# Filler matmuls placed by a shorter activity window, one K copy moved, and the closing flag put last, in a fused attention and gated-FFN kernel

## The chip, the cores and the metric

The kernel runs on one core of one Trainium2 chip. The metric is the device time of one execution in microseconds, as a median over several runs. A profiled execution gives a trace with the start and the length of every instruction of every engine; its span runs from the first to the last instruction. TensorE's clock is granted in steps, and the trace records the grant (1.0 is full speed, 0.5 half).

## What is computed

```python
xn = _layernorm(x)                       # x: 1 x 2048 x 512, bf16
q  = (xn @ wq) -> 32 heads of 16         # k, v: one head of 16 for all queries
scores = einsum("bhqd,bkd->bhqk", q, k) * 16 ** -0.5
p  = softmax(scores); o = p @ v
s  = o.reshape(...) @ wo
B  = (silu(x @ w_gate) * (x @ w_up)) @ w_down     # 1792 wide, here on xn
out = x + s * silu(B)
```

The scores are 32 heads x 2048 queries x 2048 keys, that is 134 million exponentials.

## The kernel before

**Tiles.** The score matrix is cut into 32 blocks (`NBLK`): 4 stretches of 512 queries, times 4 groups of 8 heads, times 2 halves of a group (4 heads). A block has 32 tiles of 128 keys by 2 heads by 512 queries, which is one PSUM pair of banks (128 x 1024 fp32). So there are 1024 tiles. Each tile is two score matmuls (line 877), which use 32 rows of the array each and run side by side, into one of three PSUM pairs `ring[0..2]`.

**Two engines share the exponentials.** `ring[0]` and `ring[1]` go to ScalarE, which takes 780 of the tiles with one ACTIVATE each (line 937) into one of eight buffers `Pb` (8 early tiles go into the still unused `g2_sb`, called `XB`). `ring[2]` goes to VectorE, which makes the exponential of the other 244 out of integer bit operations: a pass out of PSUM per tile (line 991), and three per two tiles (lines 1005, 1010, 1017). The products with V (line 747) are groups of four matmuls in four column strips, summed in the bank `o_ps`. The FFN, the Q projections and the output projection use the bank `m_ps`, also in groups of four (line 488).

**The order is planned in Python.** Class `_Sched` is a list scheduler that plays the engines forward with fixed costs (exponential on ScalarE 0.904 us, a group of four matmuls or one tile of scores `MMF` = 0.215, VectorE's pass out of PSUM 1.135). `pe_pick` chooses TensorE's next step: a score tile for ScalarE, a score tile for VectorE, a waiting group of another kind, or a filler. The planned order is then written out and pinned for each engine with order-only dependencies (`chain`); the semaphores come from the tile framework. Nothing is reordered at run time: each engine runs its own list and waits for data.

**Fillers.** There are three kinds. `junk` is one matmul of the identity into `ring[2]`'s second bank, used early only. `zero` is a group of four matmuls with a zero stationary operand (`zw`) that adds zero to the sums in `o_ps`. `mzero` adds zero to an open sum in `m_ps`. A filler is taken only when the plan has a gap of at least `MMF` on TensorE and `activity(F)`, the planned TensorE work in the last 3.4 us, is under `ACTMIN` = 1.7 (or, for one special case, `ACTLOW` = 1.5). A score tile counts 0.107 there, transposes (`tr`) and the narrow V projections (`vmm`, 16 columns) count nothing, everything else its length.

**Prologue.** Rows arrive in four chunks of 512. For each chunk VectorE takes statistics (lines 437, 438), GpSimd the power -1/2 (line 444), VectorE the normalised rows (447); TensorE transposes them (452); ScalarE and VectorE copy the transposes out (458); TensorE makes K (461, later 488) and V (469), and VectorE copies K out twice, masked for even and odd heads, into `KT[0]` and `KT[1]` (465). For chunk 0 these copies come in halves of 256 keys: `ke0` and `kf0` are the first half into `KT[0]` and `KT[1]`.

**Tail.** After the last exponential the sums of the last block are copied out (line 760), transposed on TensorE (1045), divided by the denominators (1053 to 1055), transposed back (1331), copied by ScalarE (1333) and multiplied by `wo` for the last four row tiles (488). VectorE multiplies by the gate (690); the residual is added by GpSimd for two row tiles and by VectorE for two (695); SyncE issues one store each (698). Beside that a flag is made: VectorE checks that the denominators lie in range (1335 to 1338), TensorE sums the result over the partitions (1343), VectorE compares (1356), and each engine loads the flag into a register (1363) and branches (1364). With the flag set, a slow exact path would redo the result; it is not taken for these inputs. All stores and the input loads go through SyncE's own queue, which issues in order.

Of the kernel before, what the change touches and what calls it, by code (L numbers as in the profile page):

```python
# [14 lines left out]
ALU = mybir.AluOpType  # L15
AX = mybir.AxisListType
# [5 lines left out]
GRP = 32  # L22
# [8 lines left out]
NWARM, NJUNK = 13, 200  # L31
D_START, D_LIM, D_LIM_END = 26, 12, 8
F_ON, F_OFF = 26, 60
PB_URG, AHEAD, LAZY, ACTMIN, ACTLOW = 6, 16, 8, 1.7, 1.5
DPRI, DTOL, DWIN = -1.0, 0.12, 0.15
TOL, MERGE, KE, KB, KR, PW = 0.17, 0.1, 1000, 3.0, 16, 2.0

# [246 lines left out]
def kernel(  # L284
# [13 lines left out]
    nc = tc.nc  # L298
    S, D, H, F = _dims(A_x, A_wq, B_w_gate)
# [38 lines left out]
    xnT = persist.tile([P, KC, S], BF16, name="xnT")  # L338
# [14 lines left out]
    ring = [psum.tile([P, 1024], FP32, name=f"ring{i}") for i in range(3)]  # L353
    o_ps = psum.tile([P, 512], FP32, name="o_ps")
    m_ps = psum.tile([P, 512], FP32, name="m_ps")
# [33 lines left out]
    zw = sb([P, GRP], BF16, "zw")  # L389
# [74 lines left out]
    def e_kev(t0, t1, src, half):  # L464
        return nc.vector.tensor_scalar(out=KT[half][:, t0:t1], in0=src, scalar1=hmask[:, half:half + 1],
                                       scalar2=None, op0=ALU.mult)
# [27 lines left out]
    def OP(eng, dur, deps, emit, prio, mode=None, name=""):  # L494
        return sd.new(_Op(eng, dur, deps, emit, prio, mode, name))
# [110 lines left out]
    ke1 = OP("DVE", 0.34, [ka1], lambda: e_kev(H2, 512, bank["o"][:, 0:H2], 0), (0.21, 0), name="kev")  # L606
    brel["2a"] = qe1
    pro_v(0, evs, "2a", 0.4)
    kf0 = OP("DVE", 0.34, [ka0, ke0], lambda: e_kev(0, H2, bank["m"][:, 0:H2], 1), (0.9, 0), name="kev")
    kf1 = OP("DVE", 0.34, [ka1, ke1], lambda: e_kev(H2, 512, bank["o"][:, 0:H2], 1), (0.25, 1), name="kev")  # L610
    brel["m"], brel["o"] = kf0, kf1
    q_ready[0] = [qe0, qe1]
# [76 lines left out]
    def e_out_mul(n, src, dst):  # L689
        return nc.vector.scalar_tensor_tensor(out=dst[:, :D], in0=src, scalar=0.25, in1=g2_sb[:, n, :],  # L690
                                              op0=ALU.mult, op1=ALU.mult)
# [5 lines left out]
    def e_out_st(n):  # L697
        return nc.sync.dma_start(out=out_v[:, n, :], in_=res[n % 4][:, :D])
# [121 lines left out]
    def act_block():  # L820
        b = cur["ba"]
        while b < NBLK and rem(b, 0) + rem(b, 1) == 0:
            b += 1
        return b if b < NBLK else None
# [309 lines left out]
    def activity(F):  # L1134
        a = 0.0
        for o in reversed(sd.pe_log):
            if o.start < F - 3.4:
                break
            a += 0.107 if o.name == "sc" else 0.0 if o.name in ("tr", "vmm") else o.dur
        return a  # L1140

    def pe_pick():
        F = sd.free["PE"]
        ready = sd.ready["PE"]
        ts = None
        b = now_block()
        rel = [i for i in (0, 1) if slot[i].start is not None]
        if b is not None and rel:
            i = min(rel, key=lambda i: sd.avail(slot[i], "PE"))
            x = act_x(b)  # L1150
            tr_ = tile_ready(b, x)
            if tr_ is not None:
                ts = max(F, sd.avail(slot[i], "PE"), tr_)
        td = None
        if d_ok() and slot[2].start is not None:
            rd = max(F, sd.avail(slot[2], "PE"))
            dt = dve_tile(1 - act_x(b) if b is not None else 0)
            if dt is not None:
                r_ = tile_ready(*dt)
                if r_ is not None:  # L1160
                    td = max(rd, r_)
        tm = None
        if ready:
            tm = max(F, min(o.ready for o in ready))
            now = [o for o in ready if o.ready <= tm + 1e-9]
            outst = cur["nA"] - sum(1 for o in pb_rel[-2 * NPB:] if o is not None and o.start is not None) \
                - max(0, len(pb_rel) - 2 * NPB)
            ba = act_block()

            def rank(o):  # L1170
                if o.name in ("pv", "dpv"):
                    fin = ba is None or o.prio[1] < ba
                    if fin or outst >= PB_URG:
                        return (0, o.prio)
                    return (1 if o.name == "dpv" else 3, o.prio)
                if o.mode == "f" or o.name == "pmm":
                    return (0.5, o.prio)
                if o.name == "part":
                    return (4, o.prio)
                return (0.8 if ahead() < LAZY else 3.5, (o.seq,))  # L1180
            co = min(now, key=lambda o: (rank(o), o.seq))
        cands = []
        if ts is not None:
            cands.append(ts)
        if tm is not None:
            if ts is None or tm + sd.switch(co.mode) + co.dur <= ts + TOL:
                cands.append(tm)
            else:
                tm = None
        if td is not None and (ts is None or td + sd.switch("r") + MMF <= ts + DTOL):  # L1190
            back = max(sd.free["DVE"] - F, 0.0) + sum(o.dur for o in sd.ready["DVE"])
            if back < DPRI and td <= F + DWIN:
                return td, ("dve", dt)
            td = None
        else:
            td = None
        junk = cur["np"] == 0 and cur["pair"] is None and cur["junk"] < NJUNK and all(
            w.start is None or v.start is not None and v.end + 0.13 <= F for w, v, bk in held if bk == "2b")
        if not cands:
            return (F, ("junk", None)) if junk else None  # L1200
        T = min(cands)
        zb = act_block()
        zb = NBLK - 1 if zb is None else zb
        act_ = activity(F)
        Tz = ts if act_ < ACTLOW and ts is not None and tm is not None and co.mode == "f" else T
        if Tz - F >= MMF + sd.switch("c") and (act_ < ACTMIN or cur["issued"] == NTILE):
            for bb in (zb - 1, zb):
                if bb >= 0 and oev[bb].start is None and oev[bb - 1].start is not None \
                        and sd.avail(oev[bb - 1], "PE") <= F and blk_pv[bb] and oev[bb].left > 0 and (bb not in fin_b or any(o.start is None for o in blk_pv[bb])):
                    return F, ("zero", bb)  # L1210
            if cur.get("mo"):
                return F, ("mzero", None)
        if junk and T - F > 0.3:
            return F, ("junk", None)
        if ts is not None and ts <= T + 1e-9:
            return ts, ("act", i)
        if tm is not None and tm <= T + 1e-9:
            return tm, ("op", co)
        return td, ("dve", dt)

    def d_ok():
        return cur["issued"] >= D_START and planned(d_gate)

    def pe_do(start, what):
# [4 lines left out]
                cur["mo"] = m_open[id(arg)]  # L1229
            return  # L1230
        if kind == "mzero":
            o = _Op("PE", MMF, [], lambda: [nc.tensor.matmul(
                out=m_ps[GRP * g:GRP * g + GRP, :], lhsT=zw[:], rhs=xnT[:, 0, 0:512], start=False, stop=False,
                tile_position=(0, GRP * g)) for g in range(4)], (0,), "c", "zero")
            o.seq = sd.seq
            sd.seq += 1
            sd.place(o, start)
            return
# [74 lines left out]
    def tadd(eng, ins):  # L1313
        chain(eng, ins)
# [1 line left out]
    la, lb = sorted((0, 1), key=lambda i: slot[i].seq)  # L1316
    assert job["part"] and job["partm"]
    st["obank"].append(f"{la}a")
    tq01, tq23 = ring[lb][:, 0:512], ring[lb][:, 512:1024]
    tp = [ring[la][:, 512:1024], o_ps[:]]  # L1320
    tadd("PE", e_out_mm(LN + 3, bank[st["obank"][3]][:, :D], range(NQ - 1)))
    tadd("PE", tq_emit(1, [0, 1], tq01))
    tadd("PE", tq_emit(1, [2, 3], tq23))
# [10 lines left out]
    dlf = dl[:].rearrange("p h q g o -> p (h q g o)")  # L1334
    tadd("DVE", nc.vector.tensor_scalar(out=dlc[:], in0=dlf, scalar1=DEN_LO, scalar2=DEN_HI, op0=ALU.max, op1=ALU.min))
    tadd("DVE", nc.vector.tensor_tensor(out=dlc[:], in0=dlc[:], in1=dlf, op=ALU.is_equal))
    tadd("DVE", nc.vector.tensor_reduce(out=fmin[:, 2:3], in_=dlc[:], axis=AX.X, op=ALU.min))
    tadd("DVE", nc.vector.tensor_reduce(out=fmin[:, 3:4], in_=fmin[:, 0:3], axis=AX.X, op=ALU.min))
    dsts = [ab[0], ab[1], oa[(LB + 1) % 4], oa[(LB + 2) % 4]]
    obk = [bank[k][:, :D] for k in st["obank"]]  # L1340
    for k in range(2):
        tadd("PE", e_out_mm(LN + k, obk[k], [NQ - 1]))
    tadd("PE", nc.tensor.matmul(out=tq01[0:1, 0:1], lhsT=fmin[:, 3:4], rhs=ones_f[:], start=True, stop=True))
    for k in range(2, 4):
        tadd("PE", e_out_mm(LN + k, obk[k], [NQ - 1]))

    def fin_add(k, eng, nm):
        tadd(nm, e_out_add(LN + k, dsts[k], eng))
        tadd("SP", e_out_st(LN + k))

    tadd("DVE", e_out_mul(LN, obk[0], dsts[0]))
    fin_add(0, nc.gpsimd, "POOL")
    tadd("DVE", e_out_mul(LN + 1, obk[1], dsts[1]))
    fin_add(1, nc.gpsimd, "POOL")
    tadd("DVE", e_out_mul(LN + 2, obk[2], dsts[2]))
    tadd("DVE", nc.vector.tensor_single_scalar(out=flag_i[:], in_=tq01[0:1, 0:1], scalar=P - 0.5, op=ALU.is_lt))
    tadd("DVE", e_out_mul(LN + 3, obk[3], dsts[3]))
    fin_add(2, nc.vector, "DVE")
    fin_add(3, nc.vector, "DVE")
    MAIN.close()  # L1360


# [34 lines left out]
```

## Time and profile before

| | |
|---|---|
| five runs, us | 784.9, 785.5, 786.14, 790.17, 792.85 (median 786.14) |
| the profiled execution's own time | 790.22 us |
| its span, first to last instruction | 788.4 us |
| mean granted TensorE clock | 0.981 |
| busy: ScalarE, VectorE, TensorE, GpSimd | 758.8, 732.3, 706.4, 50.4 us |
| ScalarE exponentials | 780 of about 1.14 us each; they overlap, and follow each other every 0.92 us |
| fillers on TensorE | 44 groups of four with zeros in `o_ps`, 7 `junk` |

The profile is a page of tables about one execution, and a trace that can be asked for more: groups of instructions by source line, waits, stretches of time, and instructions in order of time. TensorE is PE, its weight loads PEld, VectorE DVE, ScalarE ACT, GpSimd POOL, SyncE SP. A `q` behind an engine means its sequencer (waits, branches, DMA issue). "Busy" of a matmul includes its pipeline, so a busy PE is not PE at its peak.

### The profile page before, as it was taken

To read this page: it belongs to the slowest core of one execution; us is meant where nothing else is said; L and a number is where in the kernel's file an instruction comes from. 1 tells how busy PE (TensorE), PEld (TensorE's weight loads), DVE (VectorE), ACT (ScalarE), POOL (GpSimd) and SP (SyncE) were. 2 spreads that over 40 slices of the span, in tenths; PEclk is the share of its full clock that TensorE was granted. 3 is DMA by queue.
4 is the path that set the end of the run, shared out by engine and by line. 5 is a ranking of instruction groups with operands and counts; after the bars stand their busy time and mean duration, and the time that the engine had idled before them with its cause. 6 is when DMAs were issued, how large, how long until landed. Compare 5 with 4: busy or idle time off the path is not lost.

```text
span 788.4 us, 19587 instructions
## 1 busy us (share of the span) xinstructions
PE 706.4 (90%) x8170; PEld 210.4 (27%) x8172; DVE 732.3 (93%) x920; ACT 758.8 (96%) x866; POOL 50.4 (6%) x59
## 2 busy tenths in 40 slices
PE   8999888899989889899989898899988989899994
PEld 3322222222222222222222222222222222222221
DVE  7569999999989999999999999999999999999994
ACT  6889999999999999999999999999999999999993
POOL 2100000000011000000002000000000301000001
PEclk9689999999999999999999999999999999999998
DMA  9300000000011000000001000000000000000001
GB/s 328 122 22 1 23 2 15 10 2 23 3 30 42 16 15 2 22 3 10 16 18 33 29 22 2 12 13 9 17 1 23 29 23 2 1 23 2 22 2 32
DMA packets 21192, 20.09 MB, mean 25 GB/s; under 512 B 8744, under 2 KB 17192, under 8 KB 21096
## 3 DMA queue, kind: packets, MB, share of 16 engines
q1 hardware_dynamic: 19512, 18.20, 7.7%
q8 instruction: 66, 1.08, 0.6%
q10 hardware_dynamic: 1584, 0.56, 0.3%
q14 instruction: 30, 0.25, 0.1%
HBM read 14.19 MB, written 2.34 MB: 21 GB/s over the span
## 4 chain that ended last, share of the span: by engine, by line
ACT 53%; PE 28%; issue 12%; DVE 7%; DMA 0%; SPq 0%; ACTq 0%; POOL 0%; DVEq 0%; POOLq 0%
ACT Pb L937 46%; PE ring L877 10%; PE m_ps L488 10%; PE o_ps L747 5%; ACT th L657 4%; DVE Bf L991 2%; ACT th L674 1%; PE ring L433 1%; ACT g_sb L937 1%; DVE x_sb L1010 1%; DVE Bf L1010 1%; PE ring L452 0%; DVE Bf L1017 0%; DVE Bf L1005 0%; DVE x_sb L991 0%
## 5 line engine op out<-in xcount | busy, mean ns | idle before, releaser
L937 ACT ACTIVATE Pb<-ring 128x1024 bf16<-128x1024 f32 x772 | 727.0, 1136 | 8.7 <-PE ring L877 8.4
L877 PE MATMUL ring<-QB,KT 32*128 32x512 bf16 x2048 | 308.6, 387 | 60.0 <-ACT Pb L937 57.1
L991 DVE TENSOR_SCALAR Bf<-ring 128x1024 uint16<-128x1024 f32 x172 | 209.8, 1220 | 11.5 <-PE ring L877 9.7
L877 PEld LDWEIGHTS <-KT 32*128 32x128 bf16 x2048 | 92.9, 91 | 353.0 <-issue 348.9
L747 PE MATMUL o_ps<-Pb,VA 128*32 128x512 bf16 x1544 | 148.9, 388 | 0.0
L1010 DVE TENSOR_TENSOR Bf<-Bf,Bf 128x2048 f16<-128x2048 f16 x74 | 90.2, 1218 | 0.1
L991 DVE TENSOR_SCALAR x_sb<-ring 128x1024 uint16<-128x1024 f32 x72 | 87.9, 1220 | 2.4 <-PE ring L877 2.2
L488 PE MATMUL m_ps<-xnT,wu_sb 128*32 128x512 bf16 x896 | 72.8, 388 | 5.2 <-DVE ab L659 5.2
L488 PE MATMUL m_ps<-wd_sb,hT 128*32 128x512 bf16 x896 | 71.5, 383 | 1.2 <-DVE g_sb L676 1.2
L488 PE MATMUL m_ps<-xnT,wg_sb 128*32 128x512 bf16 x896 | 71.7, 385 | 0.0
L747 PE MATMUL o_ps<-Bf,VD 128*32 128x512 f16 x688 | 67.9, 387 | 0.9 <-DVE Bf L1017 0.6
L732 POOL TENSOR_TENSOR oT<-oa,rb 128x512 bf16<-128x512 f32 x15 | 20.5, 1364 | 616.3 <-DMA rb<-dscr 569.1
L1017 DVE TENSOR_SCALAR Bf<-Bf 128x2048 uint16<-128x2048 uint16 x86 | 59.2, 689 | 0.5
L747 PEld LDWEIGHTS <-VA 128*32 128x32 bf16 x1560 | 38.4, 94 | 51.5 <-issue 49.9
L1005 DVE TENSOR_SCALAR Bf<-Bf 128x2048 uint16<-128x2048 uint16 x74 | 50.6, 689 | 0.0
L659 DVE SCALAR_TENSOR_TENSOR ab<-th,m_ps 128x512 f32<-128x512 f32 x56 | 38.1, 681 | 3.4 <-ACT th L657 3.3
L663 DVE TENSOR_TENSOR hT<-ab,m_ps 128x512 bf16<-128x512 f32 x56 | 38.2, 682 | 2.5 <-PE m_ps L488 2.4
L657 ACT ACTIVATE th<-m_ps 128x512 f32<-128x512 f32 x56 | 39.8, 710 | 0.0
L747 PEld LDWEIGHTS <-VD 128*32 128x32 f16 x976 | 26.1, 94 | 41.2 <-issue 38.0
L1010 DVE TENSOR_TENSOR x_sb<-x_sb 128x2048 f16<-128x2048 f16 x24 | 30.3, 1264 | 0.0
L747 PE MATMUL o_ps<-x_sb,VD 128*32 128x512 f16 x288 | 28.0, 386 | 1.1 <-DVE x_sb L1010 0.9
L488 PEld LDWEIGHTS <-wu_sb 128*32 128x32 bf16 x896 | 19.1, 95 | 34.3 <-issue 30.5
(115 smaller groups left out, 387.9 us busy)
## 6 DMA issues: line engine op xcount, KB each, us to landing
rb<-dscr SPq DMA_DIRECT2D x15, 256.0 KB
out_dram<-xn SPq DMA_DIRECT2D x16, 128.0 KB, 1.7
dn<-oa SPq DMA_DIRECT2D x120, 2.0 KB, 1.7
oa<-oa SPq DMA_DIRECT2D x60, 32.0 KB, 2.0
wg_sb<-in_B_w_gate_dram SPq DMA_DIRECT2D x1, 1792.0 KB, 11.5
wu_sb<-in_B_w_up_dram SPq DMA_DIRECT2D x1, 1792.0 KB
wd_sb<-in_B_w_down_dram SPq DMA_DIRECT2D x1, 1792.0 KB, 20.4
x_sb<-in_A_x_dram SPq DMA_DIRECT2D x3, 512.0 KB
```

The costliest lines, as they stand in the source:

```text
L488: return [nc.tensor.matmul(out=dst[GRP * j:GRP * j + GRP, :], lhsT=w[:, GRP * j:GRP * j + GRP], rhs=rhs, start=start, stop=stop, tile_posi ...
L657: t_ = OP("ACT", 0.477, [a], lambda: nc.scalar.activation(out=th[i][:], in_=m_ps[:], func=ACT.Tanh, scale=0.5), (0,), name="tanh")
L659: s_ = OP("DVE", 0.6, [t_, ab_rel[i]], lambda: nc.vector.scalar_tensor_tensor(out=ab[i][:], in0=th[i][:], scalar=1.0, in1=m_ps[:], op0=ALU ...
L663: h = OP("DVE", 0.6, [b], lambda: nc.vector.tensor_tensor(out=hT[:, f, :], in0=ab[i][:], in1=m_ps[:], op=ALU.mult), (1,), name="hmul")
L732: return [pk, q], lambda eng: eng.tensor_tensor(out=oT[qs % 2][:, jj, :], in0=o0[:], in1=rbt[:], op=ALU.mult)
L747: r.append(nc.tensor.matmul(out=o_ps[GRP * g:GRP * g + GRP, :], lhsT=lhs, rhs=rhs, start=(n == 0), stop=(n == pv_total[(b, g)] - 1), tile_ ...
L877: return lambda: [nc.tensor.matmul(out=ring[sl][:, u * 512:(u + 1) * 512], lhsT=KT[half][GRP * g:GRP * g + GRP, t * P:(t + 1) * P], rhs=QB ...
L937: lambda: nc.scalar.activation(out=buf, in_=ring[i][:], func=ACT.Exp, scale=escale, bias=ebias),
L991: lambda: nc.vector.tensor_scalar(out=U[:, hs], in0=ring[si][:], scalar1=ubias, scalar2=UINF, op0=ALU.add, op1=ALU.min), (1.5, u), name="p ...
L1005: o1 = OP("DVE", 0.6, [pa, pa0] + wrel, lambda: nc.vector.tensor_scalar(out=Bf[wi], in0=U, scalar1=0x3FF, scalar2=0x3800, op0=ALU.bitwise_and,
L1010: return lambda: eng.tensor_tensor(out=Bf[wi][:, a:z].bitcast(FP16), in0=Bf[wi][:, a:z].bitcast(FP16), in1=U[:, a:z].bitcast(FP16), op=ALU ...
L1017: o2 = OP("DVE", 0.6, o3, lambda: nc.vector.tensor_scalar(out=U, in0=U, scalar1=0x7C00, scalar2=None, op0=ALU.bitwise_and), (2, u, 1), nam ...
```

## The change

It has five parts. (1) The planner looks back over 1.8 us in place of 3.4, and asks for 0.95 (or 0.8) of planned work in place of 1.7 (or 1.5). (2) When VectorE's score bank is free in the plan, and VectorE tiles have begun, a new filler writes zero groups into `ring[2]`'s second bank (a sum of its own, begun and closed by each group). (3) `kf0`, the copy of the first 256 keys into `KT[1]`, is planned after the last transposes of chunk 0 have been copied out. (4) In the tail the second pair of transposes goes to `o_ps` and the second transposes back go to `ring[lb]`'s second bank (the two have changed places). (5) In the tail GpSimd adds row tiles 0 and 2 and VectorE 1 and 3 (before: 0, 1 and 2, 3); the four stores stand together ahead of the flag; the flag's last two reductions, its matmul and its comparison come after the last addition.

```diff
-PB_URG, AHEAD, LAZY, ACTMIN, ACTLOW = 6, 16, 8, 1.7, 1.5
+PB_URG, AHEAD, LAZY, ACTMIN, ACTLOW = 6, 16, 8, 0.95, 0.8
...
-    kf0 = OP("DVE", 0.34, [ka0, ke0], lambda: e_kev(0, H2, bank["m"][:, 0:H2], 1), (0.9, 0), name="kev")
+    kf0 = OP("DVE", 0.34, [ka0, ke0, evs[3]], lambda: e_kev(0, H2, bank["m"][:, 0:H2], 1), (0.9, 0), name="kev")
...
-            if o.start < F - 3.4:
+            if o.start < F - 1.8:
                 break
...
             if cur.get("mo"):
+                return F, ("mzero", m_ps)
+            if d_ok() and slot[2].start is not None and sd.avail(slot[2], "PE") <= F and act_block() is not None:
                 return F, ("mzero", None)
...
-            o = _Op("PE", MMF, [], lambda: [nc.tensor.matmul(
-                out=m_ps[GRP * g:GRP * g + GRP, :], lhsT=zw[:], rhs=xnT[:, 0, 0:512], start=False, stop=False,
+            dst, own = (bank["2b"], True) if arg is None else (arg, False)
+            o = _Op("PE", MMF, [slot[2]] if own else [], lambda: [nc.tensor.matmul(
+                out=dst[GRP * g:GRP * g + GRP, :], lhsT=zw[:], rhs=xnT[:, 0, 0:512], start=own, stop=own,
...
-    tq01, tq23 = ring[lb][:, 0:512], ring[lb][:, 512:1024]
-    tp = [ring[la][:, 512:1024], o_ps[:]]
+    tq01, tq23 = ring[lb][:, 0:512], o_ps[:]
+    tp = [ring[la][:, 512:1024], ring[lb][:, 512:1024]]
...
-    tadd("DVE", nc.vector.tensor_reduce(out=fmin[:, 2:3], in_=dlc[:], axis=AX.X, op=ALU.min))
-    tadd("DVE", nc.vector.tensor_reduce(out=fmin[:, 3:4], in_=fmin[:, 0:3], axis=AX.X, op=ALU.min))
...
     for k in range(2):
         tadd("PE", e_out_mm(LN + k, obk[k], [NQ - 1]))
-    tadd("PE", nc.tensor.matmul(out=tq01[0:1, 0:1], lhsT=fmin[:, 3:4], rhs=ones_f[:], start=True, stop=True))
...
     def fin_add(k, eng, nm):
         tadd(nm, e_out_add(LN + k, dsts[k], eng))
-        tadd("SP", e_out_st(LN + k))
...
     tadd("DVE", e_out_mul(LN + 1, obk[1], dsts[1]))
-    fin_add(1, nc.gpsimd, "POOL")
     tadd("DVE", e_out_mul(LN + 2, obk[2], dsts[2]))
+    fin_add(2, nc.gpsimd, "POOL")
+    fin_add(1, nc.vector, "DVE")
+    tadd("DVE", e_out_mul(LN + 3, obk[3], dsts[3]))
+    fin_add(3, nc.vector, "DVE")
+    for k in range(4):
+        tadd("SP", e_out_st(LN + k))
+    tadd("DVE", nc.vector.tensor_reduce(out=fmin[:, 2:3], in_=dlc[:], axis=AX.X, op=ALU.min))
+    tadd("DVE", nc.vector.tensor_reduce(out=fmin[:, 3:4], in_=fmin[:, 0:3], axis=AX.X, op=ALU.min))
+    tadd("PE", nc.tensor.matmul(out=tq01[0:1, 0:1], lhsT=fmin[:, 3:4], rhs=ones_f[:], start=True, stop=True))
     tadd("DVE", nc.vector.tensor_single_scalar(out=flag_i[:], in_=tq01[0:1, 0:1], scalar=P - 0.5, op=ALU.is_lt))
-    tadd("DVE", e_out_mul(LN + 3, obk[3], dsts[3]))
-    fin_add(2, nc.vector, "DVE")
-    fin_add(3, nc.vector, "DVE")
```

Since the order is planned, a change of a threshold moves every later choice. The built programs, compared instruction by instruction, differ so: ScalarE has the same 780 exponentials and VectorE the same 244 tiles, though not all in the same order. TensorE has 56 groups of zeros in `o_ps` for 44, and 5 groups of the new kind; 7 `junk` in both. Counting ScalarE's tiles from 0: ahead of tile 32 both have 18 groups of zeros, in other places; from tile 32 to 699 there are 8 groups before, and 15 with 3 of the new kind after; from tile 700 to 778 there are 13 before, and 18 with 2 of the new kind after; behind the last score tile there are 5 in both.

## The prediction

> **What bounds the kernel now.** I read the page first: the busy row, then the clock in 40 slices.
>
> ```profile
> PE 706.4 (90%) x8170; PEld 210.4 (27%) x8172; DVE 732.3 (93%) x920; ACT 758.8 (96%) x866; POOL 50.4 (6%) x59
> ...
> PEclk9689999999999999999999999999999999999998
> ```
>
> ScalarE is the bound: its first exponential starts at 12.8 us and its last ends at 773.9, and it is busy nearly all of that. The clock row has two dips near the start and one near the end (the last slice is idle anyway). So I cut the trace at the places where the granted clock changes. Columns: stretch, its length, then busy us and (number) of PE, PEld, DVE, ACT, POOL, the clock, the DMA share and GB/s.
>
> ```profile
> 24.02:27.43 3.41, 3.05 (x40) 1.59 (x36) 3.03 (x7) 3.41 (x4) 0.61 (x3) 1.00 0.68 214
> 27.43:30.84 3.41, 3.41 (x26) 0.59 (x24) 2.08 (x6) 2.79 (x4) 1.22 (x2) 0.50 0.02 7
> ...
> 34.26:37.67 3.41, 3.41 (x22) 0.48 (x20) 0.00 (x0) 2.05 (x2) 0.00 (x0) 0.50 0.15 38
> 37.67:41.08 3.41, 3.41 (x42) 1.45 (x40) 2.06 (x4) 1.19 (x2) 0.82 (x3) 0.50 0.08 17
> ...
> 51.32:54.74 3.42, 2.33 (x28) 0.71 (x24) 3.13 (x4) 3.42 (x5) 0.00 (x0) 1.00 0.00 0
> 54.74:61.56 6.82, 6.82 (x52) 1.25 (x48) 5.14 (x6) 5.26 (x6) 0.00 (x0) 0.50 0.02 3
> ...
> 100.00:751.05 651.05, 591.67 (x6992) 173.07 (x6991) 629.96 (x741) 650.71 (x741) 36.56 (x26) 1.00 0.06 15
> 751.05:754.47 3.42, 2.18 (x26) 0.72 (x24) 3.42 (x5) 3.42 (x5) 0.00 (x0) 1.00 0.00 0
> 754.47:757.88 3.41, 3.41 (x26) 0.52 (x25) 2.48 (x4) 2.75 (x3) 0.00 (x0) 0.50 0.00 0
> ```
>
> From 100 to 751 us ScalarE idles 0.34 us in 651: nothing is to be won there. At half clock TensorE fills the whole stretch and ScalarE starves: in the four pieces from 27.43 to 41.08 it idles 0.62 + 0.97 + 1.36 + 2.22 = 5.17 us, from 54.74 to 61.56 it idles 1.56, from 754.47 to 757.88 0.66. Together **7.4 us**: all that fillers could give in this execution. The groups of instructions in the piece ahead of the first fall say why it fell:
>
> ```profile
> L877 PE MATMUL ring<-QB,KT 32*128 32x512 bf16 x8 | 1.6, 383 | 0.0
> ...
> L488 PE MATMUL m_ps<-xnT,wk_rep 128*32 128x512 bf16 x8 | 0.8, 384 | 0.0
> L452 PE MATMUL ring<-ident_bf,xn 128*128 128x128 bf16 x8 | 0.8, 220 | 0.3 <-DVE vf L474 0.3
> L469 PE MATMUL ring<-wv_sb,xnT 128*128 128x16 bf16 x16 | 0.7, 171 | 0.0
> ```
>
> Four tiles of scores, transposes, narrow V matmuls, and (by start times) one group of four wide matmuls. I counted such groups in every 3.41 us piece on this grid while the clock was full and score tiles ran (about 210 pieces): the clock fell behind three of the five with three groups or fewer (1, 3 and 3), and behind none with four or more. A piece is 3.7 exponentials, since one follows another every 0.92 us.
>
> In the tail, in order of time:
>
> ```profile
> 778.91 2.26 POOL L695 TENSOR_TENSOR xn<-ab,x_sb 128x512 bf16<-128x512 f32 x2 [33.69 <-DVE ab L690]
> ...
> 780.09 3.76 SPq L698 DMA_DIRECT2D out_dram<-xn  x4
> 780.54 1.78 DVE L695 TENSOR_TENSOR xn<-oa,x_sb 128x512 bf16<-128x512 f32 x2
> ```
>
> VectorE's last sum ends at 782.32, yet the last store is only issued at 783.48. Between stores two and three SyncE loads the flag, as the instructions of line 1363 show:
>
> ```profile
> L1363 SPq TENSOR_LOAD <-flag_i x1: 514/514/514, 781.6 to 781.6; - x1
> ```
>
> That load and the two instructions behind it hold the queue until 782.45; store three goes out at 782.56, store four at 783.48, and is waited for until 786.48; the closing handshake takes 1.92 more.
>
> **The change, part by part.** *Fillers, early.* Up to tile 32 both programs have 18 groups of zeros, so TensorE gets no more work; what counts is where. I counted groups in every four successive ScalarE tiles. Before, two such stretches have three or fewer: from tile 13 (two groups: this is the fall at 27.43) and 14 (three). After, from tiles 4 (three, and one junk), 6, 12, 13 and 23 (three each). The deep hole gets shallower, 2 to 3, and starts one tile (0.9 us) earlier; two shallow ones appear. Near tile 36, the fall at 54.74, both lists are the same. Bounds: all early falls gone, -5.17 - 1.56 = -6.7 us; one more fall, or an earlier one, +1.3 (5.17 / 4, one piece) to +5.2. I take 0, because three groups are in the range where the clock fell. The five runs support a toss of this kind: three lie at 785 to 786 and two at 790 to 793 with one fixed order of instructions; a gap of 5 to 6 us is about the price of the first fall.
>
> Here the Trainium skill speaks against any filler: "TensorE: Matmul & The Clock Gate", section "HAM oscillation", has the rule that TensorE must have no idle gap over about 3.4 us to keep its clock. The first row above is busy 3.05 of 3.41 us, and the clock fell. By the rule the fillers are worth 0 and the sum is the tail alone; by the row the kind of work matters (the same page says in Part 4 that transposes do not count as busy), and the late stretch has a gain. I go by the row.
>
> *Fillers, late.* From tile 700 there are 20 groups for 13. Stretches of four tiles with three groups: 757, 758 and 765 before, none after (the least is four). I take the fall at 754.47 as gone: **-0.66**; ends 0 and -1.3 (the hole at 765 gone too, where a run had it).
>
> *Their cost.* 17 more groups at 0.21 us (a row of 8 groups' matmuls stands at 0.61, of 12 at 0.83) are 3.6 us of TensorE, which waits 57.1 us for ScalarE at its scores anyway: 0 while that cover stands. The new kind waits for VectorE's pass over `ring[2]`, at three places; behind it on TensorE stand scores for ScalarE, which has one tile in hand. If VectorE is late there by a pass (1.22 us), less 0.9 in hand: 0.3 each, +0.9 at most. Taken 0, since the next VectorE tile waits for the same pass within a tile or two.
>
> *K copy.* VectorE's copy of the transposes does not wait for it now:
>
> ```profile
> 10.81 0.42 DVE L458 COPY xnT<-ring 128x512 bf16<-128x512 bf16 x1 [0.30 <-ACT xnT L458]
> ```
>
> It waits for ScalarE's copy until 10.78. The K copy (0.44) leaves this idle time and comes behind; the statistics of chunk 1 start up to 0.44 later. First exponential: 0. Taken 0; ends 0 and +0.44.
>
> *Tail.* The denominators' first copy waits today for all four transposes (775.66, start 775.77). With two banks it needs the first two (775.39), start 775.50: 0.27 earlier, and the chain of VectorE's steps carries that on. Products with the gate: the first starts at 778.08 - 0.27 = 777.81, then every 0.60. GpSimd's first addition 778.64 to 779.79 (1.15). VectorE's addition, ready at 779.61, would overlap. The skill's page "SBUF — State Buffer", section "Who interferes with whom", says that a VectorE instruction with two SBUF inputs contends with a reading GpSimd; the trace agrees: VectorE's addition beside GpSimd's took 1.18 us, ending 0.55 behind it, the one alone 0.67. Without the rule everything would end at 781.6 (third product's end, fourth product, addition). With it: VectorE 779.79 to 780.42, GpSimd's second to 781.57, VectorE's last 781.57 to about 782.2. Four stores then issue behind their sums: the last at 782.25 instead of 783.48, **-1.23**. The flag moves behind: two reductions 0.35, matmul 0.25, comparison 0.15 with hops, about 783.1; the load and branch another 1.1: 784.2, hidden under the last store's landing at 785.3. If that cover were gone it would still end before today's. Ends: GpSimd gets in first, VectorE's last sum at 782.8, -0.65; faster landing (1.7, as the first store's, for 3.0), -2.2.
>
> *Sum.* -1.23 - 0.66 = -1.9. The profiled execution: 788.4 + 1.8 outside the span = 790.2; after, in the same state of the clock, 788.3. The median run is 4.1 us below the profile, so most of the first fall is missing in it: 786.14 - 1.9 = **784.2 us**.
>
> **The rivals.** *(B) The early holes no longer trip.* For it: 3 groups for 2. Against: five stretches for two. The median run still pays 6.73 - 4.08 = 2.65 of the early falls; without it 781.5.
>
> *(C) The early stretch gets colder: slower than before.* Place: tiles 4 to 9 and 23 to 26, where the shorter look back lets the planner drop fillers. If most runs trip there, each pays the full early price: 790.2 - 1.9 = 788.3, with one piece more (1.3) 789.6. It decides from the third run in five on: the median moves when the share of cold runs passes a half.
>
> *(D) TensorE waits for VectorE at the new fillers*, and the late fall stays: 786.14 - 1.23 + 0.9 + 0.44 = 786.3. The 0.34 us of ScalarE's idle time in 651 says that VectorE is rarely that late.
>
> **How the numbers follow.** A 0.47, B 0.18, C 0.25, D 0.10. A's own range is 783 to 785.5. The range 781.0 to 789.7 takes in B, D and most of C; outside are B with the fast landing and C with two pieces more. Over 1% faster means under 778.3, which even all 7.4 us and the tail do not reach (790.2 - 7.4 - 2.2 = 780.6): 0.04. Over 1% slower means above 794.0, C with about four pieces more: 0.07. Within 1%, which is about what a measurement of this kernel tells from no change: 0.89.
>
> **What would show it.** Right: the clock at 1.0 from 740 us to the last matmul; the last store issued within 0.1 us of the last sum, and no flag load between stores. The early rows decide among A, B and C: where the clock first falls, and how often. Wrong: ScalarE waiting at the new fillers, a fall between 100 and 700 us, or a last sum later than 782.4 on this time axis.

## The result, and the profile after

The changed kernel takes **783.81 us** in the median (781.49 to 787.61 over 42 runs), the kernel before 786.24 over 79 runs: a ratio of 0.9965 with a 95% interval of 0.9954 to 0.9977, that is 2.4 us (1.8 to 3.6) less. The profiled execution took 784.28 us with a span of 782.5. Medians are over all runs; ratios and clocks leave out one run each of rules_late, rules_end and nofill that took over 1.5% longer than the fastest of its kernel. The forecast, 784.2, is close. The experiments show that this is partly luck: two of its terms are wrong by about 2 us each, with opposite signs.

The page of the changed kernel, with the rows that bounded the old one:

```profile
PE 702.9 (90%) x8238; PEld 211.8 (27%) x8240; DVE 732.4 (94%) x920; ACT 757.7 (97%) x866; POOL 47.9 (6%) x59
...
PEclk9999999999999999999999999999999999999998
...
L937 ACT ACTIVATE Pb<-ring 128x1024 bf16<-128x1024 f32 x772 | 726.1, 1140 | 3.1 <-PE ring L877 2.6
```

The dips in the clock row are gone, and ScalarE's exponentials waited 2.6 us for scores. In the profile of before it was 8.4:

```profile
L937 ACT ACTIVATE Pb<-ring 128x1024 bf16<-128x1024 f32 x772 | 727.0, 1136 | 8.7 <-PE ring L877 8.4
```

The changed kernel cut where the clock changes (columns as before: stretch, length, busy us of PE, PEld, DVE, ACT, POOL, then the clock):

```profile
24.02:27.43 3.41, 3.23 (x45) 1.46 (x42) 2.90 (x8) 3.41 (x5) 0.82 (x3) 1.00 0.74 236
...
119.83:123.24 3.41, 2.29 (x28) 0.70 (x21) 3.39 (x6) 3.41 (x6) 0.00 (x0) 1.00 0.13 26
123.24:126.65 3.41, 3.32 (x26) 0.64 (x25) 2.28 (x3) 2.54 (x4) 0.00 (x0) 0.50 0.09 22
126.65:775.18 648.53, 590.42 (x6987) 173.89 (x6984) 623.11 (x745) 640.38 (x728) 36.20 (x28) 1.00 0.06 15
```

There is one fall in the whole work, at 123 us, where the old profile had none; nothing falls near 27, 55 or 754. The last exponential ends at 767.18 us for 773.93. But the end of the span comes only 5.9 us earlier, so 0.8 us were lost behind the exponentials. The tail in order of time:

```profile
771.05 1.29 DVE L690 SCALAR_TENSOR_TENSOR ab<-ring,g_sb 128x512 f32<-128x512 f32 x2 [0.63 <-PE ring L488]
...
773.02 1.58 POOL L695 TENSOR_TENSOR xn<-oa,x_sb 128x512 bf16<-128x512 f32 x1
773.07 2.44 SPq L698 DMA_DIRECT2D out_dram<-xn  x4
...
774.23 0.93 DVE L695 TENSOR_TENSOR xn<-oa,x_sb 128x512 bf16<-128x512 f32 x1
...
775.79 0.15 DVE L1363 TENSOR_SCALAR flag_i<-ring 1x1 int32<-1x1 f32 x1 [0.35 <-PE ring L1362]
```

The four stores are one uninterrupted group; the fourth is issued at 775.18, 8.00 us after the last exponential's end, for 9.55 before. Its last packet lands at 776.55, and still the span ends at 782.49. What lies between are the instructions of the branch's line (columns: shortest, median and longest ns; first and last start), first in the changed kernel:

```profile
L1368 SPq EVENT_SEMAPHORE  x8: 17/17/17, 780.5 to 781.1; - x8
L1368 ACTq COMPARE_BRANCH  x1: 50/50/50, 776.5 to 776.5; - x1
...
L1368 PEldq COMPARE_BRANCH  x1: 3715/3715/3715, 776.6 to 776.6; - x1
L1368 DVEq COMPARE_BRANCH  x1: 72/72/72, 776.6 to 776.6; - x1
L1368 SPq COMPARE_BRANCH  x1: 50/50/50, 777.1 to 777.1; - x1
L1368 DVEq EVENT_SEMAPHORE  x1: 21/21/21, 779.9 to 779.9; - x1
L1368 ACTq EVENT_SEMAPHORE  x1: 17/17/17, 780.3 to 780.3; - x1
```

and then in the kernel before:

```profile
L1364 SPq EVENT_SEMAPHORE  x8: 17/17/17, 786.5 to 787.0; - x8
L1364 ACTq COMPARE_BRANCH  x1: 50/50/50, 780.6 to 780.6; - x1
...
L1364 PEldq COMPARE_BRANCH  x1: 3632/3632/3632, 780.7 to 780.7; - x1
L1364 DVEq COMPARE_BRANCH  x1: 72/72/72, 781.4 to 781.4; - x1
L1364 SPq COMPARE_BRANCH  x1: 50/50/50, 784.2 to 784.2; - x1
```

On ScalarE, VectorE and SyncE the branch takes 0.05 to 0.07 us, but the next instruction of its line starts 2.2 to 3.7 us later. On TensorE the record of the branch itself lasts 3.6 to 3.7 us; GpSimd alone goes on at once (0.12 us). Each kernel closes 1.9 us after SyncE's next instruction. The trace shows DMA packets of the kind "instruction", 8 and 16 KB, in these gaps. Before, the last of them in SyncE's gap ends at 786.60, about when SyncE goes on; in the changed kernel it ends at 778.96, and no packet of any kind moves until SyncE goes on at 780.55. So the packets suggest that the engines wait for code, but do not account for the last 1.6 us of the changed kernel's wait. Before, the branches were spread over 3.6 us and SyncE waited 2.2 us behind its own (784.26 to 786.48). After, all five engines branch within 0.7 us and SyncE waits 3.35 (777.20 to 780.55). So, counted from the last exponential: products 0.28 us earlier, last store 1.55, SyncE's branch 0.31; then the wait behind it is 1.1 longer.

### The profile page after: what moved, and what is told of

Read it like the earlier page. It is cut to its first block, busy times and chain, and to the rows that moved or that the text cites. A ratio compares the mean times of both kernels' runs of the same rounds, so it can differ in the third digit from the quotient of the medians.

```text
span 782.5 us, 19725 instructions
## 1 busy us (share of the span) xinstructions
PE 702.9 (90%) x8238; PEld 211.8 (27%) x8240; DVE 732.4 (94%) x920; ACT 757.7 (97%) x866; POOL 47.9 (6%) x59
## 4 chain that ended last, share of the span: by engine, by line
ACT 50%; PE 31%; issue 11%; DVE 7%; DMA 0%; SPq 0%; ACTq 0%; POOL 0%; DVEq 0%; POOLq 0%
ACT Pb L937 43%; PE ring L877 12%; PE m_ps L488 11%; PE o_ps L747 6%; ACT th L657 4%; DVE Bf L991 2%; ACT th L674 1%; ACT g_sb L937 1%; DVE Bf L1010 1%; PE ring L433 1%; DVE x_sb L1010 1%; DVE Bf L1017 0%; DVE Bf L1005 0%; PE ring L488 0%; DVE ab L659 0%
```

## The experiments

Two theories stood against each other. **T**, read from the trace after: the fillers gain about 3 us, and the new tail costs 0.8, since the branch and the loading of code behind it set the end. **P**, the prediction: the tail gains 1.2, as the end waits for the last store's landing, and the fillers have the rest. "Clock" below is the median over runs of the mean granted clock; the tail alone, at half clock for its last 6 to 9 us (2.5 in no_branch), keeps it below 1. Each row's ratio is against runs of before on the same chip.

| kernel | median us | ratio, 95% interval | clock |
|---|---|---|---|
| before (three comparisons) | 786.28, 786.66, 786.34 | | 0.986 to 0.987 |
| planner_only | 783.28 | 0.9962, 0.9939 to 0.9985 | 0.994 |
| tail_only | 787.69 | 1.0035, 1.0006 to 1.0063 | 0.985 |
| no_branch | 780.80 | 0.9922, 0.9894 to 0.9951 | 0.994 |
| flag_early | 783.07 | 0.9957, 0.9933 to 0.9980 | 0.994 |
| rules_early | 785.32 | 0.9984, 0.9962 to 1.0007 | 0.988 |
| rules_late | 783.15 | 0.9963, 0.9933 to 0.9993 | 0.994 |
| saturate | 799.30 | 1.0152, 1.0120 to 1.0183 | 0.996 |
| nofill | 806.06 | 1.0244, 1.0195 to 1.0294 | 0.952 |
| rules_mid | 783.89 | 0.9960, 0.9934 to 0.9985 | 0.992 |
| rules_end | 785.09 | 0.9983, 0.9956 to 1.0010 | 0.990 |
| flag_early_two_queues | 783.48 | 0.9955, 0.9931 to 0.9980 | 0.992 |
| more_fill_flag_early | 785.63 | 0.9997, 0.9973 to 1.0022 | 0.995 |

**planner_only and tail_only: the two halves.** In the first the tail (parts 4 and 5) is that of before, in the second the planner's parts (1 to 3) are. The edit of the first, against the changed kernel, begins so and goes on through the tail; the second is the reverse, made to the kernel before:

```diff
-    tq01, tq23 = ring[lb][:, 0:512], o_ps[:]
-    tp = [ring[la][:, 512:1024], ring[lb][:, 512:1024]]
+    tq01, tq23 = ring[lb][:, 0:512], ring[lb][:, 512:1024]
+    tp = [ring[la][:, 512:1024], o_ps[:]]
...
```

> The changed filler rules and the moved K copy, with the tail as it was before. Theory T (read from the changed kernel's trace: the fillers kept the clock up, and the new tail costs time, since now the branch behind the flag comes last on all engines and code has to be loaded behind it): 786.2 - 3.2 = 783.0 us, that is faster than the changed kernel by 0.8. Theory P (the prediction: the tail gains 1.23, as the end waits for the last store's landing): the fillers then have only what is left of the measured -2.4, so 785.0, slower than the changed kernel by 1.2.

> The new tail alone, with the fillers and the K copy as before. Theory T: from the last exponential's end to the end of the span 15.3 us for the 14.5 of before, so 786.2 + 0.8 = 787.0. Theory P: 786.2 - 1.2 = 785.0.

T holds for both: -3.0 us and +1.4 us. P's 785.0 is still inside the first's interval (781.5 to 785.1 us), but not inside the second's (786.8 to 791.2). The first alone is already as fast as the whole change. Of the +1.4 about 1 us is the clock, 0.985 for 0.987. The profiles give the tail by itself, from the last exponential's end to the end of the span: 14.5 to 14.9 us in the six profiles with the old tail and the usual fillers (before, planner_only and the four "rules" runs; mean 14.70), 15.32 and 15.17 in the two with the new one. So the new tail costs about **0.5 us**. Runs at the same clock say the same: at 0.994 the mean is 782.9 us before (six runs), 783.2 in planner_only (four) and 783.5 in the changed kernel (six). They also show that the fillers gain by the clock alone: at an equal clock planner_only is no faster than before.

**no_branch: what the branch costs.** It leaves out the flag's load, the branch and the exact path.

```diff
-    flag = nc.values_load(flag_i[0:1, 0:1], min_val=0, max_val=1)
-    with tc.If(flag > 0):
-        _exact_max_path(tc, nc, wo_sb, x_v, out_v, wq_sb, xnT, KT, VA, g2_sb, ident_bf, ident_f, qscale,
-                        S, D, H, NT, NQ, NSC, HD)
```

> The changed kernel without the loading of the flag, the branch and the exact path behind it (the flag is still computed, and nothing reads it). Theory T: what sets the end is the branch and the code loaded behind it, which ends 3.35 us after the branch; without it the end follows the last store's landing, seen at 776.55 for a span that ended at 782.5, plus 1.9 of closing: 778.5, so about 4.0 below the changed kernel, 779.8 us. Theory P: the flag's path is hidden under the landing, so at most 0.3 below it, 783.5 us.

3.0 us less than the changed kernel, T's direction, 1 us short of its size. In the profile the tail shrinks from 15.32 to 11.03. The stores are issued as before, the last at 774.85; its last packet lands at 776.22, SyncE starts to close at 776.95 and the span ends at 777.88. Only here does the landing set the end. The page's row of the queue that carries instructions, packets and MB, in no_branch:

```profile
q14 instruction: 25, 0.20, 0.1%
```

and in the changed kernel:

```profile
q14 instruction: 30, 0.25, 0.1%
```

With the branch go five packets of code on this queue (8 KB each), and two of 16 KB on the other that carries code. The branch and its flag load went together here, so this run does not separate the loading of code from the rest of the branch.

**flag_early: the same stores, an earlier flag.**

```diff
     tadd("DVE", nc.vector.tensor_tensor(out=dlc[:], in0=dlc[:], in1=dlf, op=ALU.is_equal))
+    tadd("DVE", nc.vector.tensor_reduce(out=fmin[:, 2:3], in_=dlc[:], axis=AX.X, op=ALU.min))
+    tadd("DVE", nc.vector.tensor_reduce(out=fmin[:, 3:4], in_=fmin[:, 0:3], axis=AX.X, op=ALU.min))
...
     for k in range(2):
         tadd("PE", e_out_mm(LN + k, obk[k], [NQ - 1]))
+    tadd("PE", nc.tensor.matmul(out=tq01[0:1, 0:1], lhsT=fmin[:, 3:4], rhs=ones_f[:], start=True, stop=True))
...
     tadd("DVE", e_out_mul(LN + 1, obk[1], dsts[1]))
+    tadd("DVE", nc.vector.tensor_single_scalar(out=flag_i[:], in_=tq01[0:1, 0:1], scalar=P - 0.5, op=ALU.is_lt))
...
+    flag = nc.values_load(flag_i[0:1, 0:1], min_val=0, max_val=1)
     for k in range(4):
         tadd("SP", e_out_st(LN + k))
```

The same five lines are taken out behind the stores.

> The changed kernel with its flag made early again (the two reductions ahead of the products with the gate, the comparison ahead of the third), while the last three stores stay together and last on SyncE. Theory T: SyncE's branch comes at about 775.9 for 777.2 on the changed kernel's axis, so 1.3 less, 782.5 us; if the code behind it also loads faster because ScalarE, TensorE and GpSimd have branched before (2.2 us for 3.35, as before the change), 781.4. Theory P: the last store is issued at the same time, so no change, 783.8.

```profile
L1368 SPq EVENT_SEMAPHORE  x8: 17/17/17, 779.5 to 780.0; - x8
L1368 ACTq COMPARE_BRANCH  x1: 50/50/50, 773.7 to 773.7; - x1
...
L1368 DVEq COMPARE_BRANCH  x1: 72/72/72, 775.6 to 775.6; - x1
L1368 SPq COMPARE_BRANCH  x1: 50/50/50, 777.1 to 777.1; - x1
```

The branches are spread again, and SyncE's wait is 2.31 us for 3.35. The last store is issued half a microsecond later than in the changed kernel (8.50 us after the last exponential for 8.00), yet the tail is 13.53 for 15.32: the last store does not set the end. The median, 783.07, is 0.7 below the changed kernel, where T has 1.3 to 2.4; the intervals of the two overlap. At a clock of 0.994 its six runs average 782.9 us for 783.5. It is faster than the kernel before.

**rules_early, rules_late, rules_mid, rules_end: where the fillers gain.** All have the old tail, the moved K copy and, throughout, the new kind of filler; the new thresholds and window hold for one stretch of score tiles only.

```diff
-        act_ = activity(F)
+        AMIN, ALOW, AWIN = (0.95, 0.8, 1.8) if cur["issued"] < 150 else (1.7, 1.5, 3.4)
+        act_ = activity(F, AWIN)
...
```

That is rules_early. rules_late has the two triples the other way round, rules_mid has the new ones from tile 150 to 900, rules_end from 900 on.

> The tail of before; the new filler rules up to score tile 150 and the old ones behind it, with the moved K copy (early 18 groups of zeros as in both kernels, behind that 11 with one of the new kind for the 8 of before, at the end 13 as before). The new rules with the old tail took 783.28 for 786.28. Theory E (the gain is in the early stretch, rival B of the prediction): 783.6. Theory L (the gain is in the middle and late stretches): 786. A spread over all stretches: about 785.

> The tail of before; the old filler rules up to score tile 150 and the new ones behind it, with the moved K copy (19 early groups, then 13 with 3 of the new kind, at the end 18 with 2). Theory E: 786, at most 0.66 less for the late fall, 785.6. Theory L: 783.5. A spread over all stretches: about 784.5.

> The tail of before; the new filler rules from score tile 150 to 900 alone (13 groups of zeros with 3 of the new kind there, for 8 before; 15 with 2 at the end for 13, since a changed plan moves what follows; none behind the last score tile). New rules from tile 150 on took 783.15, new rules up to 150 took 785.32, before 786.4 in the same comparisons. If the middle decides: 783.5. If the end decides: 785.5.

> The tail of before; the new filler rules from score tile 900 on alone (10 groups of zeros with one of the new kind in the middle, 10 with 2 at the end, 7 behind the last score tile). If the middle decides: 785.5. If the end decides: 783.5. The prediction's price for the end alone, 0.66, makes 785.7.

Theory E is out for rules_early (783.6 expected, 785.3 measured); new rules from tile 150 on give -3.5 us, as much as the new rules everywhere. Between theory L and a spread over all stretches the runs do not decide: 785.3 lies between the 786 of L and the 785 of the spread. Of the single stretches only the middle has an interval without 1 (-2.4 us by the medians); the early and the end stretch show -1.3 each, and cannot be told from nothing, nor from the middle. The three add up to more than the whole, so they are not exact shares, and rules_mid also has two groups more at the end. The medians hide one thing: 16 of 79 runs of before took over 789 us, and none of the 42 of the changed kernel, nor of the 36 of planner_only, flag_early and rules_early. That points to a gain in the early stretch, and is not tested further. rules_early, with the old rules in the middle, shows what happens there:

```profile
138.83:142.24 3.41, 2.19 (x28) 0.73 (x28) 3.22 (x5) 3.41 (x6) 0.00 (x0) 1.00 0.00 0
142.24:145.65 3.41, 3.41 (x28) 0.52 (x20) 2.66 (x4) 2.49 (x4) 0.00 (x0) 0.50 0.02 2
497.23:500.64 3.41, 2.28 (x26) 0.68 (x22) 3.41 (x5) 3.41 (x5) 0.00 (x0) 1.00 0.18 39
500.64:504.05 3.41, 3.41 (x28) 0.76 (x30) 2.59 (x5) 2.70 (x4) 0.00 (x0) 0.50 0.01 2
```

In both pairs TensorE is busy about 2.2 of 3.41 us at full clock, the next piece is at half clock, and ScalarE idles 0.92 and 0.71 us in it.

**Counting groups in all profiles.** The prediction counted groups of four wide matmuls per piece in one trace. (A wide matmul here has 128 rows, 32 columns of weights and 512 columns of data.) Here is the same count over the other thirteen, each on the grid of its own clock changes, while the clock was full and exponentials ran:

| groups in a piece | pieces behind which the clock stayed | fell |
|---|---|---|
| 2 | 2 | 7 |
| 3 | 23 | 14 |
| 4 | 77 | 5 |
| 5 and more | 2695 | 0 |

TensorE's busy time alone tells less. Of 81 pieces under 2.4 us busy, the clock fell behind 18 of the 38 with four groups or fewer and behind none of the 43 with more; and in rules_late it fell behind a piece that was busy for 3.05 us, with two groups.

The grid's phase differs from run to run (the clock is first granted at 4.4 to 7.4 us), and runs of one program differ (before: clocks of 0.975 to 0.994), so what an order of instructions sets is a chance. Sliding a 3.41 us piece over 100 to 700 us in the traces, away from stretches at half clock, the length of the starting points with three groups or fewer, in units of a piece, is 1.2 to 1.4 with the old rules in the middle (before, tail_only, rules_early, rules_end), and 0.4 to 0.5 with the new (changed kernel, planner_only, rules_late, rules_mid). So the new rules leave fewer thin pieces in the middle, whatever a run's luck. The size does not follow: by the table a piece with three groups trips in 14 of 37, and with some 1.2 us for each half-clock piece (worked out below) 0.8 fewer such pieces make about 0.4 us, an estimate, for the 2.4 measured.

**nofill and saturate: the fillers' two ends.** No group of zeros ahead of the last score tile; and one in every planned gap. Both have the old tail.

```diff
-PB_URG, AHEAD, LAZY, ACTMIN, ACTLOW = 6, 16, 8, 0.95, 0.8
+PB_URG, AHEAD, LAZY, ACTMIN, ACTLOW = 6, 16, 8, -1.0, -1.0
```

That is nofill, against planner_only; saturate has 9.0 and 9.0. The rule of the idle gap in the two expectations is the one that the prediction cites.

> The tail of before; the new rules with a limit that is never met, so no groups of zeros ahead of the last score tile (before has 39 there). Theory F: more falls than before, among the early tiles and towards the end; 39 groups fewer for 17 more that gained 3.0, so 790 to 795, clock 0.98 or less. By the rule of the idle gap: TensorE still has none near 3.4 us, so 786.3.

> The tail of before; the new rules with no limit on recent activity, so a filler goes into every planned gap that holds one (337 groups of zeros for 56, and 8 of the new kind). Theory F (the number of groups of four wide matmuls in a 3.4 us stretch decides, so fillers keep the clock up, and they cost nothing while TensorE waits for ScalarE): no fall of the clock ahead of the tail, about 782. Rival (fillers delay the scores): ScalarE waits more than 5 us for them, 785 or more. By the rule that only an idle gap over 3.4 us lets the clock fall, fillers change nothing and the result is that of before, 786.3.

Without fillers the time is 19 us more, beyond what was expected. The clock row of nofill (its profile is of its longest run, 815.2 us, so only the places of the falls count):

```profile
PEclk9559999999969999999998999999999899999658
```

With a filler in every gap the clock never falls ahead of the tail, and the time is 13 us more than before all the same. ScalarE in saturate:

```profile
L937 ACT ACTIVATE Pb<-ring 128x1024 bf16<-128x1024 f32 x774 | 727.7, 1141 | 15.3 <-PE ring L877 13.6 <-PE o_ps L747 1.5
```

Seven waits for scores make the 13.6 us, three of them of 4 us at 27, 39 and 50 us. The tail is longer too, 17.1 us for 14.7. The expectation of 782 was wrong: a filler in a gap costs nothing only while nothing else comes due behind it.

**flag_early_two_queues and more_fill_flag_early: can it be better still?**

```diff
-        tadd("SP", e_out_st(LN + k))
+        tadd("ACT" if k < 2 else "SP", e_out_st(LN + k, nc.scalar if k < 2 else nc.sync))
```

That is two_queues, on flag_early; ScalarE issues the first two stores. more_fill is flag_early with limits of 1.05 and 0.9 in place of 0.95 and 0.8 from score tile 60 on (114 groups for 56).

> The changed kernel with the flag made early, as in the run flag_early, and the first two of the last four stores issued by ScalarE (idle by then) in place of SyncE, so that SyncE loads the flag ahead of its first store and only two stores and the branch are left to it. In flag_early SyncE branched at 777.13, 1.25 behind the last sum's end at 775.88. Theory T: SyncE's branch comes 0.5 us earlier and the end with it, 783.07 - 0.5 = 782.6, from the last exponential to the end 13.0 us for 13.5 and 15.3 in the changed kernel. Rival: the end then hangs on VectorE's own branch and its code (775.6 to 778.4 in flag_early), so 783.0.

> The changed kernel with the flag made early, and from score tile 60 on a limit of 1.05 for 0.95 (0.9 for 0.8): 114 groups of zeros for 56, 3 of the new kind for 5. If fillers still cost nothing at this number and the last falls of the clock go: the clock at 0.996 in every run, as with no limit at all, and 781.7, about what the coldest-free runs of flag_early took. If they delay the scores, as with no limit (799.3, with 15 us of waiting on ScalarE): above 784.

Two queues show no gain in the median: SyncE branches 0.27 us earlier (8.96 us behind the last exponential for 9.23), but ScalarE and VectorE then branch within 1.6 us of it and its wait grows from 2.31 to 2.68. More fillers lose 2.6 us against flag_early in the medians. In the profile no fall is left in the work, but ScalarE idles 3.2 us between 100 and 700 us for 1.5, with one wait of 2.0 us for a product with V, and the tail is 0.85 longer. No run beats flag_early for certain; in the median it is the fastest that computes everything.

## Why the prediction was right, and where it was wrong

The number held because two errors cancel. The sum was -1.23 (tail) - 0.66 (fillers) = -1.9. The runs show about +0.5 and -3.0, and -2.4 for both together.

- **The tail is the step that failed.** It said of the last store that it "is waited for until 786.48", and that the flag and the branch, at 784.2, are "hidden under the last store's landing at 785.3". The old trace already spoke against it: the store's last packet landed at 785.32, 1.2 us ahead of SyncE's next instruction at 786.48. That instruction takes up the stores' semaphores, but the trace has the last of them raised by 785.71: what SyncE had just done was to branch (until 784.26). In no_branch, where the landing does decide, SyncE goes on 0.73 us after the last packet (776.22 to 776.95). By that the old landing was done by 786.05, so an earlier one alone had nothing to gain, and even without the wait behind the branch the landing would have let the end come only 0.4 us sooner. The term left out is that wait, 2.2 us when the branches are spread and 3.35 when all engines branch together; no_branch shows that it goes with the branch. That it is the loading of code is inferred from the packets. The Trainium skill has the rule that was not weighed: "Runtime: NRT & Kernel Launch", section "Instruction fetch mechanics", says that a taken branch to a target outside the window at hand must fetch its code before the engine goes on. The packets of instructions in the gaps agree with it, up to the 1.6 us without any in the changed kernel; the page gives no time for it. "If that cover were gone it would still end before today's" is wrong too.
- **The steps ahead of the flag were right.** The products start 0.28 us earlier (0.27 predicted), the last store is issued within 0.03 us of the last sum, 8.00 us behind the last exponential (8.3 predicted); the branch comes at 9.97 (10.3 predicted). GpSimd's second addition took 1.58 us beside VectorE's, not 1.15, at no cost.
- **"Nothing is to be won there" (100 to 751 us) is the other wrong term.** It took one execution, in which the two middle pieces with three groups (at 324 and 683 us) happened to keep the clock, for the rule. By its own count such pieces fell three times in five. Its own sign of being wrong, a fall between 100 and 700 us, came at 123 us. rules_mid has a gain of 2.4 us (interval 1.2 to 5.2) that the sum lacks; the thin pieces explain its direction, not its size. One half-clock piece lowers a run's mean clock by 3.41 / 2 / 784 = 0.0022; before, runs at 0.981 took 790.0 us and runs at 0.994 took 783.0, so a piece costs about 1.2 us, and 0.987 to 0.993 is some three pieces a run.
- **Fillers early, 0, and late, -0.66:** both lie in the intervals of rules_early and rules_end, and neither is settled. Rival B (781.5) has a filler gain of 3.3, near the 3.0 measured, but puts it in the early stretch, and its tail is wrong. Rival C (colder early) did not come about.
- **The fillers' cost, 0,** holds for these 17: at equal clock (0.994) planner_only is within 0.3 us of before, by four runs and six. It does not hold for 58 more (more_fill_flag_early). The prediction's "a row of 8 groups' matmuls" is a row of 8 matmuls, two groups, and 12 are three; its 0.21 us a group is the difference of the two and stands. Rival D falls; the new kind waited for no engine, as its line shows in the changed kernel:

```profile
L1235 PE MATMUL ring<-xnT,zw x20: 378/379/390, 447.2 to 747.1; 128*32 128x512 bf16 x20
...
  issue: 0.5, 2
```

- **The K copy, 0,** holds: the first exponential starts at 12.80 us for 12.78, VectorE's statistics 0.41 later, as said.
- **Row against rule for the clock:** the row was right. By the rule of the idle gap fillers are worth nothing; taking them out cost 19 us. The two falls of rules_early shown above follow pieces in which TensorE is busy 2.2 of 3.41 us, so no gap in them exceeds 1.2. In the profiles of before, rules_early and tail_only, with all their falls, TensorE's longest gap between matmuls while exponentials ran is 1.02 us, in nofill 1.19.

Three things stay open. The first is how the filler gain divides among the stretches. The second is what the engines wait for in the part of the changed kernel's gap in which no code moves. The third is why flag_early's tail is 1.8 us shorter in the profile and its median only 0.7 lower: in its profile ScalarE also idled 0.6 us more after 700 us, and no repeat of that profile was taken. It is not the clock, as the runs at 0.994 differ by 0.6 too; no_branch likewise has a tail 4.3 us shorter for 3.0 us of time.

## What to carry to other kernels

When a transfer seems to set the end, compare the time of its last packet with the time at which the engine goes on; if they differ, look at what the engine did in between, branches above all, and try to spread the engines' branches (as flag_early did), or put them where something else is still running. Where the clock depends on a window whose phase nobody sets, count over all phases of the program how often the window is thin, and not what one execution happened to pay. A filler is free until something is due behind it, so add the few that thin stretches need.

## What the runs showed of the hardware

The 0.05 us branch past a long block of code cost SyncE 1.9 to 3.4 us in thirteen profiles, and most where the engines branched closest together:

| kernel | SyncE's branch behind VectorE's, us | SyncE's wait behind its branch, us |
|---|---|---|
| planner_only | 2.8 | 2.47 |
| before | 2.8 | 2.22 |
| flag_early | 1.5 | 2.31 |
| flag_early_two_queues | 1.1 | 2.68 |
| tail_only | 0.5 | 3.20 |
| changed kernel | 0.5 | 3.35 |

In the seven other profiles SyncE's branch is 2.4 to 3.2 us behind, and its wait 1.91 (nofill) to 2.70 (saturate), so the order does not hold among the spread ones. That the engines' code loads share a path is a guess from these numbers and was not tried by itself; it does not explain the stretch without packets. Second, the clock fell 26 times in the thirteen profiles other than before, behind pieces of full clock, nine of them in nofill, and never behind one with five groups or more (2695 pieces). In this kernel that number tells more than TensorE's busy time does.
